# Windowed attention and a gated convolution layer: the first two units' softmax in six parts of two blocks, with other PSUM banks and other planned times

## The chip, the core and the metric

The kernel runs on one core of one Trainium2 chip. The metric is the device time of one execution in microseconds (us); the median of three runs stands for a kernel. The engines are named as in the profile: PE is TensorE (matrix products), PEld its weight loads, DVE is VectorE, ACT is ScalarE, POOL is GpSimd, SP is SyncE, which here only issues transfers (DMA).

## What is computed

```python
def _attn_ref(q, k, v):                       # [8, 8, 576, 64] each
    scores = scale * np.matmul(q, k.transpose(0, 1, 3, 2))
    mask = (rel >= 0) & (rel < 64)            # rel = query place - key place
    scores = np.where(mask, scores, -1000000000.0)
    scores = scores - np.max(scores, axis=-1, keepdims=True)
    attn = np.exp(scores)
    attn = attn / (np.sum(attn, axis=-1, keepdims=True) + 1e-09)
    return np.matmul(attn, v)
...
def _moe_ref(x, w_in, conv_w, w_out):         # x [8, 576, 512], w_in [512, 1024]
    h = np.maximum(x @ w_in, 0.0)
    ...
    for k in range(3):                        # over neighbouring tokens, zeros at a sequence's ends
        conv_out += conv_w[k][None, None, :] * hp[:, k:k + S, :]
    gate = 1.0 / (1.0 + np.exp(-conv_out))
    return h * gate @ w_out
```

Each token attends to itself and the 63 before it, in 8 heads of 64. The three weight arrays come as 64-bit floats, everything else as 32-bit floats.

## The kernel before

**Units.** The 8 x 576 tokens are cut into 12 units (`u`) of 384 tokens, six blocks of 64. For each unit the kernel makes the attention output, splits it in a high and a low half (`xh`, `xl`), multiplies by `w_in`, applies the three-tap convolution and the gate, splits the gated values (`gh`, `gl`) and multiplies by `w_out`.

**The two large products.** Both weights are split in high and low parts too (`wih`, `wil`, `woh`, `wol`), and every product is the sum of three: high by high, high by low, low by high. `mm1` (L512) makes one of eight output strips `f` of a unit with 12 products into a bank of `acc`; `mm2` (L574) adds one strip `f` into the four banks `po` with 12 more. That is 2 x 8 x 12 products a unit, 2304 in all. `relu` on ACT empties `acc` into `hbuf`, of which there are two, so unit u+2 writes over what unit u left. A pair of strips then goes through `conv_mid` (ACT), `conv_side` (DVE, four instructions), `sig` (ACT), `gate` (DVE), `gate_hi` (ACT) and `gate_lo` (DVE), with two buffers `c` and three of `gh` and `gl`.

**Weights.** Each strip of `w_in` arrives as 512 KB of raw 64-bit words in `bits` (`weights`, L258). `to_f32` (L246) makes floats of them with two ACT and three DVE instructions (L250 to L256), POOL or ACT copies out the high half, and a DVE subtraction (L274) leaves the low half `wil` or `wol`. Strips 0 and 1 go alone, later ones in pairs. `mm1` of strip f can't run before its `wil` is there.

**Attention.** A unit has two groups `g` of heads with six blocks each, twelve in all, taken in three sets `b` of four. Scores (`qk`) go to PSUM, DVE takes the row maxima and adds the mask (`row_max`, L363), ACT makes the exponentials and their sums (`exps`, L373), POOL adds 1e-9 to the sums (`guard`, L376), DVE inverts them (L379) and multiplies (`normalise`, L384). In units 0 and 1 PE then transposes the result into `po` (`transpose_pe`, L390) and ACT copies it to `ub` (`untile`, L395); in later units DVE and transfers do that. `values` (L495) multiplies by v into a bank of `acc`, and `split_hi` (ACT, L499) and `split_lo` (DVE, L502) leave `xh` and `xl`. All four strips of `xl` are needed before the first `mm1` of a unit can end. In units 0 and 1 a set of four blocks uses two PSUM banks: for unit 0 those are `sc`, then `po` 2 and 3, then `po` 0 and 1; for unit 1 always `sc`.

**Order.** Nothing is ordered by the loop nest. Every step is put in a list with a due time (`at`, L220), an engine, a cost and the names that it reads and writes; due times come from the table `START` (L139), in units of one `mm1` strip. `queued` (L59) goes through the list with its own costs and writes each engine's instructions in one fixed order, which the chip then follows; each engine works its queue in that order and waits where a name isn't ready. Where PE would stand idle early on, `keep_busy` (L209) puts in products of a zero tile `spare` (L214) that nobody reads.

The two entries that say most about that order:

```python
    "lag": (5.734, 4.983, 5.01, 5, 4.601, 6.631),    # mm2 of strip f is due so many strips after mm1 of it
    "sig": ((5.726, 6.552, 8.72, 10.544), ...        # the sigmoid of pair i is due so many strips after its unit's first
```

Of the kernel before, what the change touches and what calls it, by code (L numbers as in the profile page):

```python
# [30 lines left out]
NBU = 2 * NT // NB  # L31
MASKED = -8.0e9
# [26 lines left out]
def queued(works, fill=None):  # L59
# [80 lines left out]
    "v0": -45.616,  # L140
    "pv0": -37.371,
    "conv": -174.861,
    "bits": ((-210.989, -90.898), (-76.132, -86.24)),
    "qk1": -82.37,
    "lag": (5.734, 4.983, 5.01, 5, 4.601, 6.631),
    "mid": (0.325, 6.316, 0.269, 99),
    "v1": -1.517,
    "qk2": -29.766,
    "qk0": (-93.532, -87.041, -82.642),
    "ex0": (-76.037, -72.861, -50.81),  # L150
    "sc1": (-59.709, -43.924, -30.076),
    "ex1": (-36.764, -20.322, -18.147),
    "mask": -51.623,
    "sig": ((5.726, 6.552, 8.72, 10.544), (1.673, 4.482, 8.678, 7.763), (4.834, 5.504, 8.278, 8.811), (4.046, 6.806, 8.285, 10.314)),
    "in": (-91.819, -70.332, -46.356, -13.522, -9.317),
    "out": (5.121, 7.311, 7.45, 11.284),
# [13 lines left out]
def attention_moe(ctx: ExitStack, tc: tile.TileContext, q, k, v, w_in, conv_w, w_out, out):  # L170
# [57 lines left out]
    def load_qk(t, u, gs=(0, 1)):  # L228

        for g in gs:  # L230
            c, n = slice(2 * g, 2 * g + 2), (4, 2)[g] * W
            cut = (0, n + W, NX + W), (0, n, NX)
            for a in ((0, 1), (1, 2)) if u == 0 else ((0, 2),):
                for name, sb, dram, ends in (("k", ks, k, cut[0]), ("q", qs, q, cut[1])):
                    e = slice(ends[a[0]], ends[a[1]])
                    at(t, "SP", 0.5, lambda c=c, e=e, sb=sb, dram=dram: nc.sync.dma_start(sb[:, c, e], dram[u, :, c, e]),  # L236
                       w=[(name, g, i) for i in range(*a)], mb=(0.00145 if u == 0 else 0.00112) * (e.stop - e.start))
# [66 lines left out]
    def wide(u):  # L304
        return u < BY_PE
# [31 lines left out]
    def halves_of(name, i):  # L337
        return [(name, i, 0), (name, i, 1)]

    def banks_of(u, b):  # L340
# [410 lines left out]
```

## Time and profile before

| | before |
|---|---|
| median of 3 runs | 522.91 us (520.26 to 523.6) |
| the profiled execution's own time | 519.87 us |
| its span, first to last instruction | 517.9 us |
| granted TensorE clock, mean | 0.998 |
| first `mm1` product starts | 34.88 us |
| first `mm2` product starts | 66.77 us |
| DVE busy, 34.9 to 59.4 us | 24.10 of 24.5 us |
| DVE busy, 250 to 450 us | 145.76 of 200 us |

Times in the profile count from the span's first instruction. A row of the timeline gives the start, the length, the engine, the line, the operation, what it writes and reads with shapes, how many instructions are merged, and in brackets how long the engine stood idle before it and what ended that. Instructions of one engine overlap at their ends, so the cost of one among others is the distance to the next one's start. The chain of waits goes back from the last instruction; its pieces don't overlap. In a row of busy times by stretch the columns are the length, the busy time of PE, PEld, DVE, ACT and POOL with instruction counts, the granted clock, the share of the DMA engines and GB/s.

### The profile page before, as it was taken

How to read it: one execution, taken by the hardware profiler on the slowest of the kernel's cores; microseconds unless marked ns; L12 is line 12 of the kernel's file. 1: busy time of each engine (PE TensorE's matmuls, PEld its weight loads, DVE VectorE, ACT ScalarE, POOL GpSimd, SP SyncE). 2: the span in 40 equal slices, each digit the busy share in tenths (PEclk: the TensorE clock that was granted, in tenths of full speed). 3: DMA queues.
4: the chain of work that ended last, by engine and by line, in shares of the span. 5: the costliest groups of instructions: out<-in, count | busy, mean ns of one | idle time of the engine just before them, and what ended most of it. 6: DMA issues, size and time to landing. Idle time of an engine off the chain costs nothing.

```text
span 517.9 us, 14661 instructions
## 1 busy us (share of the span) xinstructions
PE 508.0 (98%) x5742; PEld 488.4 (94%) x5742; DVE 372.4 (72%) x1084; ACT 382.8 (74%) x1015; POOL 85.4 (16%) x186
## 2 busy tenths in 40 slices
PE   9899899999999999999999999999999999999996
PEld 8788899999999999999899999899899999999996
DVE  4799998986787785766668877677677578554550
ACT  5989797979995894894796895795795696444440
POOL 7123131003030120130121130130130021000000
PEclk9999999999999999999999999999999999999999
DMA  8974923152382461462272451362272043010011
GB/s 294 380 274 171 350 80 117 62 176 76 127 291 69 145 218 47 138 208 66 96 255 60 161 202 49 123 234 55 86 260 65 3 153 121 1 62 2 0 62 61
DMA packets 29460, 69.95 MB, mean 135 GB/s; under 512 B 5712, under 2 KB 17616, under 8 KB 29392
## 3 DMA queue, kind: packets, MB, share of 16 engines
q1 hardware_dynamic: 29392, 69.03, 39.3%
q8 instruction: 45, 0.74, 0.6%
q14 instruction: 23, 0.19, 0.1%
HBM read 47.73 MB, written 9.47 MB: 110 GB/s over the span
## 4 chain that ended last, share of the span: by engine, by line
PE 82%; DVE 9%; DMA 5%; ACT 1%; issue 1%; SPq 1%; ACTq 0%
PE po L580 38%; PE acc L515 33%; PE acc L495 6%; PE sc L356 5%; DMA q<-in_q_dram 2%; DVE s L363 2%; DMA bits<-in_w_out_dram 1%; DVE s L384 1%; DVE T L252 1%; DVE T L256 1%; DMA k<-in_k_dram 1%; DVE c L563 1%; DVE wil L274 1%; DVE xl L502 1%; SPq L236 1%
## 5 line engine op out<-in xcount | busy, mean ns | idle before, releaser
L580 PE MATMUL po<-gh,woh 128*128 128x386 f32 (+1 forms) x384 | 132.4, 345 | 0.0
L515 PE MATMUL acc<-xh,wih 128*128 128x384 f32 x384 | 130.7, 340 | 0.6 <-ACT hbuf L534 0.6
L580 PE MATMUL po<-gh,wol 128*128 128x386 f32 (+1 forms) x384 | 130.0, 339 | 0.0
L580 PE MATMUL po<-gl,woh 128*128 128x386 f32 (+1 forms) x384 | 129.7, 338 | 0.1
L515 PE MATMUL acc<-xh,wil 128*128 128x384 f32 x384 | 129.0, 336 | 0.3 <-issue 0.3
L515 PE MATMUL acc<-xl,wih 128*128 128x384 f32 x384 | 128.8, 335 | 0.0
L551 DVE SCALAR_TENSOR_TENSOR c<-hbuf,cw,c 128x386 f32<-128x386 f32 (+1 forms) x192 | 111.9, 633 | 22.5 <-ACT c L544 22.4
L373 ACT ACTIVATE s<-s,nm 128x96 f32<-128x96 f32 (+2 forms) x288 | 105.1, 368 | 3.4 <-DVE nm L363 3.2
L580 PEld LDWEIGHTS po<-gh,woh 128*128 128x128 f32 x384 | 72.2, 188 | 2.9
L515 PEld LDWEIGHTS acc<-xh,wih 128*128 128x128 f32 x384 | 72.1, 188 | 2.7 <-ACT hbuf L534 1.1
L580 PEld LDWEIGHTS po<-gl,woh 128*128 128x128 f32 x384 | 72.4, 188 | 0.4 <-DVE gl L571 0.4
L515 PEld LDWEIGHTS acc<-xh,wil 128*128 128x128 f32 x384 | 72.1, 188 | 0.5 <-issue 0.5
L580 PEld LDWEIGHTS po<-gh,wol 128*128 128x128 f32 x384 | 72.2, 188 | 0.0
L515 PEld LDWEIGHTS acc<-xl,wih 128*128 128x128 f32 x384 | 72.1, 188 | 0.0
L563 DVE TENSOR_TENSOR c<-c,hbuf 128x772 f32<-128x772 f32 (+1 forms) x48 | 47.0, 982 | 31.2 <-ACT c L558 30.8
L571 DVE TENSOR_TENSOR gl<-c,gh 128x772 fp32r<-128x772 f32 (+1 forms) x48 | 51.8, 1082 | 22.1 <-ACT gh L567 21.8
L384 POOL TENSOR_TENSOR s<-s,r 128x768 f32<-128x768 f32 x27 | 40.4, 1496 | 152.1 <-DVE r L379 138.8
L363 DVE CUSTOM_DVE_ANT_0 s<-sc,mask 128x96 f32<-128x96 f32 (+2 forms) x272 | 51.9, 257 | 16.8 <-PE sc L356 16.8
L373 ACT ACTIVATION_READ_ACCUMULATOR s<-s,nm 128x1 f32 x288 | 54.6, 190 | 0.0
L558 ACT ACTIVATE c<-c 128x772 f32<-128x772 f32 (+1 forms) x48 | 40.6, 847 | 18.8 <-DVE c L551 18.6
L567 ACT CAST gh<-c 128x772 fp32r<-128x772 f32 (+1 forms) x48 | 40.0, 834 | 18.4 <-DVE c L563 13.7
L544 ACT ACTIVATE c<-hbuf,cw 128x386 f32<-128x386 f32 (+1 forms) x96 | 53.5, 608 | 0.0
(63 smaller groups left out, 551.9 us busy)
## 6 DMA issues: line engine op xcount, KB each, us to landing
v<-in_v_dram SPq DMA_DIRECT2D x24, 768.0 KB, 6.4
ub<-T SPq DMA_DIRECT2D x240, 48.0 KB, 1.9
k<-in_k_dram SPq DMA_DIRECT2D x22, 448.0 KB, 6.2
q<-in_q_dram SPq DMA_DIRECT2D x22, 384.0 KB, 7.0
out_dram<-T SPq DMA_DIRECT2D x8, 772.0 KB, 3.8
bits<-in_w_in_dram SPq DMA_DIRECT2D x8, 512.0 KB, 6.1
bits<-in_w_out_dram SPq DMA_DIRECT2D x8, 512.0 KB, 6.6
out_dram<-T SPq DMA_DIRECT2D x3, 768.0 KB, 4.6
```

Of the source, the lines that this page charges most:

```text
L363: nc.vector.tensor_tensor_reduce(out=ss[b][:, i, h, o:n], in0=banks_of(u, b)[h][:, i * P + o:i * P + n], in1=mask[m][:, o:n], scale=-0.125 ...
L373: nc.scalar.activation(x, x, AF.Exp, bias=nms[b][:, e], scale=-1.0, accum_out=sms[b][:, e])
L384: on.tensor_tensor(sv, sv, rs[b].unsqueeze(2).broadcast_to([P, 2 * NB, n]), ALU.mult)
L495: nc.tensor.matmul(acc[bank(("v", u, c))][h * D:(h + 1) * D, t * W:(t + 1) * W], vs[:, c, t, h], ub[g][:, 2 * p:2 * p + 2, 2 * t + h], sta ...
L515: nc.tensor.matmul(acc[bank(("m", u, f))][:, :NX], w[:, f, c], x[u % 2][:, c], start=(c == 0 and j == 0), stop=(c == NC - 1 and j == 2))
L544: nc.scalar.activation(cs[i % 2][:, a, :n], hbufs[u % 2][:, f, 1:1 + n], AF.Copy, scale=cw[:, 1, f:f + 1])
L551: nc.vector.scalar_tensor_tensor(c, hbufs[u % 2][:, f, e:e + n], cw[:, e, f:f + 1], c, op0=ALU.mult, op1=ALU.add)
L558: nc.scalar.activation(c, c, AF.Sigmoid)
L563: nc.vector.tensor_tensor(c, c, hbufs[u % 2][:, 2 * i:2 * i + 2, 1:1 + n], ALU.mult)
L567: nc.scalar.copy(ghs[ring(u, i)][:, :, :n], cs[i % 2][:, :, :n])
L571: nc.vector.tensor_tensor(gls[ring(u, i)][:, :, :n], cs[i % 2][:, :, :n], ghs[ring(u, i)][:, :, :n].bitcast(F32), ALU.subtract)
L580: nc.tensor.matmul(po[o][:, :n], w[:, f, es], x, start=(f == 0 and j == 0), stop=(f == NF - 1 and j == 2))
```

## The change

Units 0 and 1 lose `softmax`; in its place `scores` and `weigh` work in six parts of two blocks. `scores` plans the score products and row maxima of one part; `QK_AT` names its banks (-1 is `sc`, 0 is `po` 0 and 1, 2 is `po` 2 and 3). `weigh` plans exponentials, guard, reciprocal, normalisation, transposes and copies for a group of parts: parts 0 and 1 together, 2 alone, 3 alone, 4 and 5 together. So there are four guards, reciprocals and normalisations a unit where there were three; blocks, maxima, exponentials, transposes and copies keep their number. `PE_AT` names the bank of `po` for each part's transposes. The loads of q and k are cut after two of six blocks in both groups (before: after four in the first group, two in the second). The planner knows `po` banks by one name each where it had two halves. All due times in `START` are new; `lag` goes from about 5 to 16 to 18, which puts `mm2` two units behind `mm1`.

```diff
+NP = 2 * NBU
+CUTS = ((2, 6), (2, 6))
+GROUPS = ((0, 1), (2,), (3,), (4, 5))
+QK_AT = (((-1,), (0,), (2,), (-1,), (0,), (2,)), ((-1,), (2,), (-1,), (2,), (-1,), (2,)))
+PE_AT = ((0, 1, 2, 3, 0, 1), (0, 1, 0, 1, 0, 1))
...
-    "lag": (5.734, 4.983, 5.01, 5, 4.601, 6.631),
+    "lag": (16.159, 16.007, 16.941, 17.14, 18.073, 17.348),
...
-    "sig": ((5.726, 6.552, 8.72, 10.544), (1.673, 4.482, 8.678, 7.763), (4.834, 5.504, 8.278, 8.811), (4.046, 6.806, 8.285, 10.314)),
+    "sig": ((12.206, 13.508, 18.787, 21.562), (12.436, 17.352, 18.346, 20.414), (14.01, 17.284, 19.69, 20.122), (15.611, 16.37, 18.929, 20.186)),
...
+    def scores(u, n, t):
+
+        b, bl = n // 2, range(n % 2 * 2, n % 2 * 2 + 2)
+        for i in bl:
+            if block(u, b, i)[1]:
+                at(t - 0.1, "POOL", 0.2, lambda i=i: nc.gpsimd.memset(ss[b][:, i, :, :W], 0.0), w=[("s", b, i)])
+        at(t, "PE", 0.45, lambda: qk(u, b, bl), r=needed(b, bl), w=keys_of(u, b, bl[0]), kind="tiled")
+        for i in bl:
+            at(t + 0.002 + 0.001 * (i % 2), "DVE", 0.42, lambda i=i: row_max(u, b, (i,)),
+               r=keys_of(u, b, i) + ["mask0"], w=[("s", b, i), ("nm", b, i)])
+
+    def weigh(u, ns, t):
+
+        bis = [divmod(2 * n + i, NB) for n in ns for i in range(2)]
+        for b, i in bis:
+            at(t, "ACT", 0.78, lambda b=b, i=i: exps(u, b, i), r=[("nm", b, i)], w=[("s", b, i), ("sm", b, i)], kind="exp")
+        t += 0.45
+        b = bis[0][0]
+        e = slice(2 * bis[0][1], 2 * bis[-1][1] + 2)
+        sw, sr = [("sm", b, i) for _, i in bis], [("s", b, i) for _, i in bis]
+        at(t, "POOL", 0.6, lambda: guard(b, e, nc.gpsimd), w=sw)
+        at(t, "DVE", 0.15, lambda: reciprocal(b, e), r=sw, w=[("r", b, i) for _, i in bis])
+        two(t, "DVE", 0.05 + 0.275 * len(bis), lambda: normalise(u, b, e, nc.vector), r=[("r", b, i) for _, i in bis], w=sr)
+        for n in ns:
+            m, g = [("po", PE_AT[u][n])], 2 * n // NT
+            at(t + 0.4, "PE", 0.66, lambda n=n: transpose_pe(u, n), r=[("s", b, n % 2 * 2), ("s", b, n % 2 * 2 + 1), "mask0"], w=m)
+            at(t + 0.5, "ACT", 0.55, lambda n=n: untile(u, n), r=m, w=[("u", g, i) for i in range(4)])
...
-    for b in range(NBU):
-        softmax(0, b, START["qk0"][b], START["ex0"][b])
+    for n in range(NP):
+        scores(0, n, START["qk0"][n])
+    for ns in GROUPS:
+        weigh(0, ns, START["ex0"][ns[-1]])
```

What the table does is seen in the order of the instructions. PE, just ahead of the first `mm1` (`s_81` holds the first four blocks of unit 1's softmax, `ub_62` the second group of unit 0's). Before:

```order
L495 MATMUL acc_107<-ub_62,v 64x64 x12
L495 MATMUL acc_108<-ub_62,v 64x64 x12
L214 MATMUL po_111<-spare 128x112 x3
L390 MATMUL po_109<-ident,s_81 128x128 x4
L390 MATMUL po_110<-ident,s_81 128x128 x4
L515 MATMUL acc_107<-xh_63,wih 128x384
```

and now, where the score rows of parts 4 and 5 of unit 1 are shown by the last two of part 5:

```order
L522 MATMUL acc_107<-ub_62,v 64x64 x12
L522 MATMUL acc_108<-ub_62,v 64x64 x12
...
L371 MATMUL po_111<-k,q 64x128
L371 MATMUL po_112<-k,q 64x128
L219 MATMUL po_109<-spare 128x112 x2
L542 MATMUL acc_107<-xh_63,wih 128x384
```

The transposes of unit 1 moved from ahead of the first `mm1` to behind it, and all of unit 1's scores stand ahead of it in both.

DVE, around the last two `xl` of unit 0 (`T` is the weights' work buffer, `wil` a low half of `w_in`). Before:

```order
L256 ISA T<-bits_103,T 128x2048
L384 TENSOR_TENSOR s_81<-s_81,r_90 128x1024
L502 TENSOR_TENSOR xl_65<-acc_107,xh_63 128x384
L502 TENSOR_TENSOR xl_65<-acc_108,xh_63 128x384
...
L274 TENSOR_TENSOR wil<-T,wih 128x1024
```

and now:

```order
L262 ISA T<-bits_102,T 128x1024
L529 TENSOR_TENSOR xl_65<-acc_107,xh_63 128x384
L529 TENSOR_TENSOR xl_65<-acc_108,xh_63 128x384
...
L399 TENSOR_TENSOR s_81<-s_81,r_90 128x1024
L394 RECIPROCAL r_91<-sm_88 128x4
...
L399 TENSOR_TENSOR s_82<-s_82,r_91 128x512
L280 TENSOR_TENSOR wil<-T,wih 128x512
L280 TENSOR_TENSOR wil<-T,wih 128x1024
```

The normalisation of unit 1 moved behind `xl`, and so did the low half of weight strip 1 (the row of 512), which before was made long ahead.

PE, where the first `mm2` stands (`gh_95` is the first pair's gated half; `po_109` is the first of four banks). Before, after strip 1 of unit 1 was half done:

```order
L515 MATMUL acc_108<-xl_66,wih 128x384
L580 MATMUL po_109<-gh_95,woh 128x386
...
L580 MATMUL po_112<-gl_98,woh 128x386
L515 MATMUL acc_108<-xh_64,wih 128x384
```

and now, after all eight strips of unit 1:

```order
L542 MATMUL acc_108<-xl_66,wih 128x384
L607 MATMUL po_109<-gh_95,woh 128x386
...
L607 MATMUL po_112<-gl_98,woh 128x386
L522 MATMUL acc_107<-ub_61,v 64x64 x12
```

All 192 `mm1` products of the first two units now stand ahead of the first `mm2`, where 114 did.

More of the change, by code (lines that the diff above doesn't have):

```diff
@@ L456, in softmax @@
+        sw, sr = [("sm", b, i) for i in range(NB)], [("s", b, i) for i in range(NB)]
         if u < 3:
-            at(t, "POOL", 0.6, lambda b=b: guard(b, nc.gpsimd), w=sw)
+            at(t, "POOL", 0.6, lambda: guard(b, e, nc.gpsimd), w=sw)
         else:
-            at(t, "DVE", 0.15, lambda b=b: guard(b, nc.vector), w=sw)
-        at(t, "DVE", 0.15, lambda b=b: reciprocal(b), r=sw, w=[("r", b)])
-        sr = [("s", b, i) for i in range(NB)]
+            at(t, "DVE", 0.15, lambda: guard(b, e, nc.vector), w=sw)
@@ L466, in softmax @@
         t += 0.4
-        if u < BY_PE:
-            for j in range(2):
-                m, g = halves_of("po", (2 * b + j) % NC), place_of(b, NB // 2 * j)[0]
-                at(t, "PE", 0.66, lambda b=b, j=j: transpose_pe(b, j), r=sr + ["mask0"], w=m)
-                at(t + 0.1, "ACT", 0.55, lambda b=b, j=j: untile(b, j), r=m, w=[("u", g, i) for i in range(4)])
-            return
         t = max(t, when[-1][2] + 0.1)
```

136 lines of the change are left out of this document (69 added, 67 removed), and 6 rows, old and new, of the table START.

## The prediction

> **What bounds the kernel now.** The page comes first: the span, and the chain that ended last by engine.
>
> ```profile
> span 517.9 us, 14661 instructions
> ...
> PE 82%; DVE 9%; DMA 5%; ACT 1%; issue 1%; SPq 1%; ACTq 0%
> ```
>
> PE ends the kernel, but a DVE and a DMA part lie on the chain. Where, the busy times by stretch say (PE, PEld, DVE, ACT, POOL; then clock, DMA share, GB/s).
>
> ```profile
> 22.20:34.90 12.70, 11.41 (x183) 9.83 (x183) 11.29 (x52) 10.07 (x38) 2.93 (x3) 1.00 0.75 259
> 34.90:59.40 24.50, 22.93 (x444) 20.26 (x441) 24.10 (x84) 21.93 (x63) 7.63 (x16) 1.00 0.71 265
> 59.40:77.00 17.60, 17.60 (x161) 17.00 (x158) 17.21 (x37) 16.89 (x35) 4.11 (x9) 1.00 0.42 145
> 77.00:120.00 43.00, 42.25 (x431) 40.31 (x431) 37.35 (x84) 35.71 (x80) 2.95 (x8) 1.00 0.40 130
> ...
> 250.00:450.00 200.00, 200.00 (x2398) 193.41 (x2397) 145.76 (x443) 153.80 (x413) 32.76 (x55) 1.00 0.37 125
> ```
>
> To 59 us DVE has hardly a gap; from there PE has none but 0.75 us. The timeline of PE shows when useful work starts, and the rates.
>
> ```profile
> 31.78 1.62 PE L495 MATMUL acc<-ub,v 128*64 128x64 f32 x48
> ...
> 34.09 1.04 PE L390 MATMUL po<-ident,s 128*128 128x128 f32 x8
> 34.88 0.42 PE L515 MATMUL acc<-xh,wih 128*128 128x384 f32 x1
> ...
> 37.15 0.99 PE L356 MATMUL sc<-k,q 64*32 64x96 f32 x64
> ...
> 66.77 0.33 PE L580 MATMUL po<-gh,woh 128*128 128x386 f32 x1
> ...
> 73.08 0.44 PE L515 MATMUL acc<-xh,wih 128*128 128x384 f32 x1
> ```
>
> And from the chain over the whole span, in the steady part and at the end:
>
> ```profile
> 199.64 2.12 PE acc L515 x12
> 201.76 2.10 PE po L580 x12
> ...
> 496.89 16.96 PE po L580 x96
> ```
>
> A strip of 12 products takes 2.10 us, 0.175 a product, whichever of the two it is. From 34.88 us on PE works almost without pause, so the end can only move by what the head gives, or by what new pauses take. The measure: how many of the 2304 large products are done at a given time. By the order, 114 `mm1` stand ahead of the first `mm2`, then 24 `mm2` and 6 `mm1`, and from 73.08 to 76.9 us run 3.8 us of `mm1`, some 20.5 with the change-overs: 164.5 in all.
>
> **The start, to the first mm1.** The chain of waits in the head:
>
> ```profile
> 9.54 11.57 DMA q<-in_q_dram
> ...
> 21.15 1.07 PE sc L356 x32
> ...
> 22.50 0.20 DVE s L363
> 22.70 0.01 DVE nm L363
> ...
> 24.55 0.14 DVE s L363
> ...
> 26.50 1.14 DVE T L252
> ...
> 31.48 1.13 DVE T L256
> 32.62 1.14 DVE s L384
> 33.75 0.93 DVE xl L502 x2
> ```
>
> Unit 1's q lands at 21.11 us, its first row maximum runs at 22.2, the last `xl` of unit 0 ends at 34.7. Between those two DVE also normalises `s_83` of unit 0 and `s_81` of unit 1 and makes two passes over weights: four times 1.14 us that now stand elsewhere. Now there are 16 maxima there, 14 of 128 columns at 0.21 and two of 64 at 0.15 (3.2 us), the weight pass of strip 1 (half of 1.13, 0.6) and four `xl` (1.9): 5.7 us.
>
> When does that stretch start? Two things set it. The transfers:
>
> ```profile
> 7.00:15.00 8.00, 8.00 (x139) 7.16 (x138) 6.62 (x53) 6.36 (x33) 4.37 (x27) 1.00 1.05 384
> ...
> bits<-in_w_in_dram SPq DMA_DIRECT2D x8, 512.0 KB, 6.1
> ```
>
> The DMA engines are full at 384 GB/s. On SP one 512 KB strip more stands ahead of unit 1's q (five where four did): 1.3 us, so q lands at 22.4 and the first maximum can run at 23.4. The other is ACT, which now has all 24 exponentials ahead of the first `untile`, then the first pass over strips 2 and 3.
>
> ```profile
> 16.71 0.56 ACT L395 COPY ub<-po 128x512 f32<-128x512 f32 x1
> ...
> 19.00 1.05 ACT L395 COPY ub<-po 128x512 f32<-128x512 f32 x2
> ...
> 20.72 1.13 ACT L250 ACTIVATE T<-bits 128x1024 f32<-128x1024 f32 x1
> ```
>
> A copy among others costs 0.47 us, a pass over two strips 1.04. The strips now stand behind both loads of v; up to the landing of q at 21.1 the queue before moved 6104 KB, up to that of strip 3 it now moves 4736 (strip 0, all of unit 0's q and k, both v, strips 2 and 3). That is 1368 KB less, 3.5 us at 384 GB/s: 17.6. Pass 1.04, three copies 1.4, the pass over strip 1 0.56, a copy 0.47, the other pass over strips 2 and 3 1.0: 22.1 us. Then DVE's third pass over them, 1.13: 23.4. Both ways give 23.4; 5.7 more, and the last `xl` of unit 0 ends at 29.1 where it ended at 34.7. That gain of 5.6 us is not yet the kernel's: work was put behind it.
>
> **From there to the second unit.** Up to the last `xl` of unit 1 DVE now has these rows: 12 full-width weight passes and normalisations (1.14 each, 13.7), three shifts L251 (0.56, 1.7), three pieces of half width (1.8), 6 maxima of 128 columns, 2 of 64 and 32 of 96 (7.2), four `xl` (1.9), and normalisations of 768, transposes, reciprocals and the convolution's small weights (4.4, an estimate by their widths): 30.7 us. The widths not shown yet:
>
> ```profile
> 36.98 0.65 DVE L251 TENSOR_SCALAR T<-T 128x1024 uint32<-128x1024 uint32 x1
> 37.53 1.22 DVE L384 TENSOR_TENSOR s<-s,r 128x1024 f32<-128x1024 f32 x1
> 38.67 0.26 DVE L363 CUSTOM_DVE_ANT_0 s<-sc,mask 128x96 f32<-128x96 f32 x1
> ...
> 40.09 1.23 DVE L252 SCALAR_TENSOR_TENSOR T<-bits,T 128x1024 uint32<-128x1024 uint32 x1
> ```
>
> (0.55 from the first to the second; eight maxima of 96 in 1.42.) PE follows DVE in this stretch, so each DVE wait counts. Two are added. The first is the low half of strip 1, now behind its copy on POOL, and a POOL copy beside a normalisation is slow:
>
> ```profile
> 32.69 1.96 POOL L273 CAST wih<-T 128x1024 fp32r<-128x1024 f32 x1 [5.21 <-DVE T L256]
> ...
> 45.46 1.04 POOL L273 CAST wih<-T 128x1024 fp32r<-128x1024 f32 x1 [1.08 <-DVE T L256]
> ```
>
> The first of these ran beside the normalisation at 32.62, the second did not: 0 to 0.9 us, and I take 0.9, since the two again stand side by side. The Trainium skill has the rule for it (SBUF — State Buffer, Terms, "shared port pair": DVE and GpSimd lock it for a whole instruction, the loser waits). By that rule the split into four normalisations gives a guard four chances a unit to be held for up to one of them; the trace bears out the hold, and the sum would lose at most another 1.1 us.
>
> The second wait is what DVE idled in the same stretch before (24.10 of 24.50): 0.4. So the last `xl` of unit 1 ends at 29.1 + 30.7 + 0.9 + 0.4 = 61.1 us. Strips 0 to 7 of unit 0 are done by then: their 16.8 us, four `values` of 0.8, four score groups of 0.95 and the transposes, 0.4 a part and 2.4 in all, make 26.2 us of PE work between 29.1 and 61.1. Of unit 1 only the second half of strip 0 and seven strips remain, 90 products, 15.75 us with nothing to wait for but ACT. At 76.9 us 192 products are done, against 164.5: 27.5 x 0.175 = 4.8 us ahead. Scores, values and transposes done are the same in both at that time, and so the 0.9 us of transposes that went behind the first `mm1` is in it.
>
> **After that** PE has all it needs if the gates keep up. The first pair's `gl` comes 13.9 us of DVE rows after the last `xl` of unit 1, at 75.0, and is wanted at 76.9. The third pair's comes 37.1 us after it, at 98.2; PE wants it after 4.2 + 2.6 + 1.1 + 0.5 of `mm2`, 10.5 of `mm1`, four `values` (3.2) and two score groups (1.9), at 100.9. Both margins are about 2 us: the cover is there, and thin. In the steady part the work per unit is the same, the number of product groups changes little, and the tail is the same copy and transfer behind PE's last product. Two entries cost nothing: one name for a bank instead of two removes no instruction, and the spare products that go, 16 of 63 rows, lie where PE waits.
>
> The sum: 517.9 - 4.8 = 513.1 us of span. The profiled execution took 519.87 us, 2.0 more than its span; the median of the runs shown is 522.91, another 3.0. The same 4.8 from the median: 518.1.
>
> **Rivals.**
>
> *More is gained* (0.17). If POOL's copy meets no normalisation, DVE doesn't idle, and the strips land with the first v (768 KB, 2.0 us earlier, with q at 22.4 still the later end, so 0 from that), 0.9 + 0.4 return, and the 0.75 us that PE lost from 77 to 120 may go, a few shorter regroupings on PE besides: 6.1 to 7.5, median 516.1. For it: 24.10 of 24.5 shows how few gaps DVE can have.
>
> *The head gives less* (0.24). ACT's fixed order puts copies that PE waits for behind strips still in transit. Each microsecond that strips 2 and 3 land later than 17.6 moves 23.4 and all behind it; the 6.1 us from issue to landing is a median under such load. With 2 us later, or the same lost in the thin margins up to 100 us, 2.8 remain; with 4.8, none: median 520.1 to 522.9.
>
> *Slower* (0.13). `relu` of unit u+2 may not write `hbuf` before `gate` of unit u has read it, and with `mm2` two units behind, the gate is near that limit in every unit. The chain of one pair is 0.6 + 0.6 on ACT, four `conv_side`, `sig` and `gate`. From the group means,
>
> ```profile
> L551 DVE SCALAR_TENSOR_TENSOR c<-hbuf,cw,c 128x386 f32<-128x386 f32 (+1 forms) x192 | 111.9, 633 | 22.5 <-ACT c L544 22.4
> L558 ACT ACTIVATE c<-c 128x772 f32<-128x772 f32 (+1 forms) x48 | 40.6, 847 | 18.8 <-DVE c L551 18.6
> L563 DVE TENSOR_TENSOR c<-c,hbuf 128x772 f32<-128x772 f32 (+1 forms) x48 | 47.0, 982 | 31.2 <-ACT c L558 30.8
> ```
>
> 1.2 + 2.5 + 0.85 + 1.0 = 5.6 us. For the fourth pair PE gives it about six strips, 13 us, from the freeing of its `c` to the next use of the `acc` bank. DVE is busy 29 of 40 us a unit, so in 13 us it has 9.4 of work, 3.5 of it this pair's; 5.9 of others' plus 5.6 is 11.5. From 1.5 us more on PE pauses in each of ten units; 1 us each is 10 us: 513.1 + 10, median 528.1. Against it: a quarter of DVE is free, and what `relu` waits for is PE:
>
> ```profile
> ACT hbuf L538 <- PE acc L515: 27.5, 24, 2.6
> ```
>
> *The clock* (0.03). Fewer spare products before the first `mm1` could let the granted clock fall; one strip at half clock costs 2.1 us, median 520.2. Before, the clock is 1.00 in each stretch quoted. The Trainium skill (TensorE: Matmul & The Clock Gate, What's actually happening) has the clock halved after an idle window of about 3.4 us; no run here shows that.
>
> **Chances and range.** The forecast as summed, 3 to 6 us gained, has 0.43. A median of three runs of this kernel tells 1% (5.2 us) from no change at best. Faster by over 1% is the rival with more gain and two fifths of the forecast: 0.35. Slower is 0.13; the rest, 0.52, is within 1%. The range goes from 514.5 (a gain of 7.5 and 1 us of scatter) to 523.5 (no gain, and some scatter); the slower rival and some of the clock's lie outside. The forecast's own range is 516.9 to 519.9.
>
> **What would show it.** First `mm1` near 29 us and its last `xl` at 29.1; last `xl` of unit 1 at 61; first `mm2` at 77; no pause of PE over 0.5 us from 61 on. A first `mm2` at 80 or later says the head gave less; PE waiting for `hbuf` or `gl` in every unit after 120 us is the slower rival. The forecast is wrong at its root if the stretch before 61 isn't carried by DVE's rows, or PE's steady rate isn't 0.175.

## The result, and the profile after

The changed kernel takes 517.08 us (median of 15 runs, 515.53 to 520.81) where the kernel before takes 520.52 on the same chip (15 runs, 519.0 to 523.6). The ratio is 0.9936, with a 95% interval of 0.9913 to 0.9958: 3.3 us gained, 2.2 to 4.5 by the interval. Beside the last experiment the changed kernel was timed again: 516.98 against 519.96, ratio 0.9952 (0.9933 to 0.9971). The profiled execution took 516.12 us, its span is 3.6 us shorter than before's. The 522.91 us from which the forecast started is the median of the first three of before's 15 runs, 2.4 us above the median of all.

From the page of the changed kernel, the span and the chain by engine:

```profile
span 514.3 us, 14601 instructions
...
PE 89%; DVE 5%; ACT 2%; DMA 2%; issue 0%; SPq 0%; DVEq 0%; ACTq 0%
```

PE's share of the chain rose from 82 to 89%, DVE's fell from 9 to 5% and that of DMA from 5 to 2%: less of the chain lies on DVE's rows and on transfers. The busy times by stretch of the changed kernel (PE, PEld, DVE, ACT, POOL; then clock, DMA share, GB/s):

```profile
22.20:29.40 7.20, 6.64 (x148) 5.81 (x152) 6.83 (x39) 6.64 (x26) 1.90 (x3) 1.00 0.87 294
29.40:61.00 31.60, 29.82 (x557) 27.02 (x555) 30.30 (x117) 29.94 (x107) 9.12 (x21) 1.00 0.71 251
...
77.00:120.00 43.00, 41.32 (x623) 39.37 (x623) 38.17 (x134) 37.37 (x117) 8.89 (x14) 1.00 0.47 150
120.00:250.00 130.00, 130.00 (x1439) 126.40 (x1438) 89.65 (x262) 101.01 (x263) 23.01 (x40) 1.00 0.40 131
250.00:450.00 200.00, 199.97 (x2279) 193.83 (x2278) 137.42 (x405) 146.65 (x379) 31.26 (x53) 1.00 0.36 114
```

Up to 61 us DVE has little room, and so has ACT (29.94 of 31.6 us, which the prediction did not look at). After 120 us PE is full, as before. But from 77 to 120 PE now lacks 1.68 us where it lacked 0.75. The timeline of DVE in the head, and of PE from the first `mm1` on:

```profile
23.86 0.28 DVE L378 CUSTOM_DVE_ANT_0 s<-sc,mask 128x128 f32<-128x128 f32 x1
...
28.63 1.02 DVE L529 TENSOR_TENSOR xl<-acc,xh 128x384 fp32r<-128x384 f32 x2
...
32.98 1.83 DVE L280 TENSOR_TENSOR wil<-T,wih 128x512 fp32r<-128x512 f32 x2
...
38.16 0.69 DVE L257 TENSOR_SCALAR T<-T 128x1024 uint32<-128x1024 uint32 x1 [1.17 <-ACT T L256]
...
60.98 0.55 DVE L529 TENSOR_TENSOR xl<-acc,xh 128x384 fp32r<-128x384 f32 x1
61.45 0.95 DVE L399 TENSOR_TENSOR s<-s,r 128x768 f32<-128x768 f32 x1
```

```profile
30.32 0.42 PE L542 MATMUL acc<-xh,wih 128*128 128x384 f32 x1
...
33.59 0.99 PE L371 MATMUL sc<-k,q 64*32 64x96 f32 x64 [0.94 <-DMA q<-in_q_dram]
...
77.53 0.33 PE L607 MATMUL po<-gh,woh 128*128 128x386 f32 x1
...
83.55 1.62 PE L522 MATMUL acc<-ub,v 128*64 128x64 f32 x48 [1.64 <-ACT hbuf L561]
```

The last row is the new pause: 1.64 us, waiting for a `relu` of ACT to free `acc`. What ACT did then:

```profile
79.10 1.15 ACT L256 ACTIVATE T<-bits 128x1024 f32<-128x1024 f32 x1 [2.11 <-DMA bits<-in_w_out_dram]
...
83.04 0.83 ACT L561 ACTIVATE hbuf<-acc 128x384 f32<-128x384 f32 x2
```

ACT stood 2.11 us in front of strips of `w_out` still in transit. The two `relu`, whose products PE had ended at 75.6 and 77.7, are behind that pass, a gate copy and six exponentials in ACT's order.

The sum goes like this. At 77.53 us the changed kernel has done 192 large products. The kernel before had 164.5 at 76.9, so 168.1 at 77.53, and 23.9 products of 0.175 us are 4.2 us. Counted in the traces it is 23, since the kernel before has begun 169 by then; the score and value products still to come are the same in both, 1600 and 960. To 120 us the changed kernel loses 0.93 us more than the one before (1.68 - 0.75), and after that neither loses anything. That leaves 3.3 of the 3.6 us between the two spans; where the rest comes from was not traced.

### The profile page after: what moved, and what is told of

Same layout as the page of the kernel before. It is cut to its first block, busy times and chain, and to the rows that moved or that the text cites. A ratio compares the mean times of both kernels' runs of the same rounds, so it can differ in the third digit from the quotient of the medians.

```text
span 514.3 us, 14601 instructions
## 1 busy us (share of the span) xinstructions
PE 504.4 (98%) x5710; PEld 487.0 (95%) x5710; DVE 367.0 (71%) x1088; ACT 380.0 (74%) x1013; POOL 91.2 (18%) x188
## 4 chain that ended last, share of the span: by engine, by line
PE 89%; DVE 5%; ACT 2%; DMA 2%; issue 0%; SPq 0%; DVEq 0%; ACTq 0%
PE po L607 40%; PE acc L542 36%; PE acc L522 6%; PE sc L371 5%; DVE s L378 2%; PE acc L219 1%; DMA bits<-in_w_out_dram 1%; DVE T L262 1%; ACT T L256 1%; DMA q<-in_q_dram 1%; PE po L371 1%; DVE wil L280 1%; DVE s L399 1%; ACT ub L409 0%; DVE xl L529 0%
## 5 line engine op out<-in xcount | busy, mean ns | idle before, releaser
L399 POOL TENSOR_TENSOR s<-s,r 128x768 f32<-128x768 f32 x27 | 41.8, 1547 | 231.0 <-DVE r L394 180.4
L598 DVE TENSOR_TENSOR gl<-c,gh 128x772 fp32r<-128x772 f32 (+1 forms) x48 | 47.3, 986 | 22.8 <-ACT gh L594 21.9
L378 DVE CUSTOM_DVE_ANT_0 s<-sc,mask 128x96 f32<-128x96 f32 (+2 forms) x260 | 49.1, 254 | 16.0 <-PE sc L371 15.5
L565 ACT ACTIVATE hbuf<-acc 128x384 f32<-128x384 f32 x64 | 30.9, 484 | 28.3 <-PE acc L542 28.3
```

Source lines behind the costliest of these rows:

```text
L378: nc.vector.tensor_tensor_reduce(out=ss[b][:, i, h, o:n], in0=bank_of(u, b, i, h)[:, o:n], in1=mask[m][:, o:n], scale=-0.125, scalar=3.0e3 ...
L399: on.tensor_tensor(sv, sv, rs[b][:, e].unsqueeze(2).broadcast_to([P, e.stop - e.start, n]), ALU.mult)
L565: nc.scalar.activation(hbuf[:, f, o:o + NX], ps[:, :NX], AF.Relu)
L598: nc.vector.tensor_tensor(gls[ring(u, i)][:, :, :n], cs[i % 2][:, :, :n], ghs[ring(u, i)][:, :, :n].bitcast(F32), ALU.subtract)
```

## The experiments

In the kernels of this table the order of the engines is that of the changed kernel except for the instructions named, because the edit moves them in the planner's finished list. Where planned times or the code of the parts change, the planner orders everything anew. The kernels were timed on several chips, each beside the kernel before, so the ratios compare better than the medians.

| kernel | median us | ratio to before (95%) | first `mm2` at, us | span behind it, us |
|---|---|---|---|---|
| changed kernel | 517.08 | 0.9936 (0.9913 to 0.9958) | 77.53 | 436.8 |
| the same, again | 516.98 | 0.9952 (0.9933 to 0.9971) | 76.86 | 437.8 |
| relu first | 516.42 | 0.9929 (0.9916 to 0.9943) | 78.28 | 437.4 |
| strips first | 516.14 | 0.9930 (0.9912 to 0.9948) | 79.28 | 435.6 |
| scores behind | 516.24 | 0.9930 (0.9906 to 0.9954) | 78.42 | 436.2 |
| both moves | 515.95 | 0.9928 (0.9902 to 0.9954) | 81.38 | 436.7 |

The last two columns are from each kernel's one profiled execution. "Scores behind" has the strips moved too.

### What the pause at 83.5 us costs

First the two `relu` were moved on ACT:

```diff
...
+late = [x for x in order if x.eng == "ACT" and x.t < 16 and x.w in ([("h", 1, 6)], [("h", 1, 7)])]
+order = [x for x in order if x not in late]
+i = next(n for n, x in enumerate(order) if x.eng == "ACT" and x.t == START["out"][3])
+order[i:i] = late
...
```

> The changed kernel with two entries of ACT's order moved: the relu of the last two strips of unit 1 stand ahead of ACT's pass over the strips of w_out that land at 79 us, and so ahead of a gate copy and six exponentials too; nothing else moves. Theory (the head gave what was forecast, and 1.64 us of it was lost again at 83.55 because ACT stood in front of a transfer): the pause of PE at 83.5 goes to under 0.3 us, the span falls from 514.3 to 512.7 us, 5.2 below before's 517.9, and the median by as much (515.4 where the changed kernel has 517.1). Rival (the margins behind are used up: what PE takes next, the low halves of the gate or the weights, is late anyway): the pause turns up a few us later, span within 0.5 of 514.3.

Measured: 516.42 us, and a span of 515.7 in the profile. The pause was not gone but had moved by one step of PE's order. PE and ACT of this run:

```profile
85.51 1.16 PE L371 MATMUL sc<-k,q 64*32 64x96 f32 x64 [1.30 <-DVE nm L378]
```

```profile
80.23 1.12 ACT L256 ACTIVATE T<-bits 128x1024 f32<-128x1024 f32 x1 [1.25 <-DMA bits<-in_w_out_dram]
```

Now PE waits for row maxima, which stand behind the same weight pass in DVE's order. The rival was right for this run: PE's 77 to 120 us hold 41.32 us of work again. (Only its span missed the rival's figure, since in this execution PE also waited 2.46 us for unit 2's q at 39.8.) So not ACT's order alone but the landing of the strips is the cause, and the next run moves that. On SP, k and q of unit 3 were issued ahead of those strips:

```diff
...
+late = [x for x in order if x.eng == "SP" and 15 < x.t < 15.9 and x.w and x.w[0][0] in ("k", "q") and x.w[0][1] == 0]
+order = [x for x in order if x not in late]
+i = max(n for n, x in enumerate(order) if x.eng == "SP" and x.w and x.w[0][:2] == ("bits", 1))
+order[i + 1:i + 1] = late
...
```

> The changed kernel with one move in SP's order: the two strips of w_out that ACT waits for at 79 us are issued ahead of k and q of unit 3 (832 KB) instead of behind them; PE, DVE, ACT and POOL as in the changed kernel. Theory (ACT and DVE both stood in front of that transfer, and so the last relu and the next row maxima came late): the strips land about 2 us earlier, at 77 (832 KB at the 400 GB/s moved there), PE's pause at 83.5 goes, and with it no other one of over 0.5 us appears up to 120 us; 1.6 us off the span of a like execution, median about 515. Rival (the strips are late because their buffer comes free late, or the other transfers slow them all the same): they land within 0.5 us of 79, and the time is that of the changed kernel.

The strips landed at 78.96 in an execution whose first `mm2` was 1.75 us later than that of the changed kernel, so 1.9 us earlier against the rest of the work. By the absolute time alone this is what the rival had said; from the issue on SP to ACT's pass it now took 5.2 us instead of 6.7. ACT and the stretch of PE:

```profile
78.96 1.14 ACT L256 ACTIVATE T<-bits 128x1024 f32<-128x1024 f32 x1 [0.21 <-DMA bits<-in_w_out_dram]
```

```profile
77.00:120.00 43.00, 42.79 (x633) 40.91 (x632) 39.70 (x134) 39.06 (x122) 10.62 (x14) 1.00 0.51 168
```

PE lacks 0.21 us where it lacked 1.68, and the span behind the first `mm2` is 1.2 us shorter. The pause is gone by the mechanism named, and it stays away in the two other profiles with this move ("scores behind" and "both moves"), where ACT doesn't wait for these strips at all. The median, 516.14, is 0.9 under that of the changed kernel, or 0.3 by the ratios, which these two intervals do not tell from nothing. The head of this execution was late, with 1.84 us of waiting for unit 2's q at 40.8, and hid the gain in the span. Both moves together were therefore timed beside the changed kernel on one chip:

> The changed kernel itself, beside the run below on the same chip: 517.1 us as before, pause of PE of 1.6 us near 83.5.

> The changed kernel with both moves that bear on the pause at 83.5: the strips of w_out ahead of k and q of unit 3 in SP's order, and the last two relu of unit 1 ahead of ACT's pass over them. Theory (1.2 to 1.6 us of the forecast gain were lost at that place, and the rest of what was missing is scatter of the transfers in the head): no pause of PE over 0.5 us between 77 and 120, the part of the span behind the first mm2 under 435.9 us (changed kernel 436.8), median 1.2 to 1.6 under that of the changed kernel on the same chip. Rival (the head's scatter hides it, or the place costs less than its pause): under 0.6 us.

The changed kernel showed its pause again:

```profile
82.83 1.62 PE L522 MATMUL acc<-ub,v 128*64 128x64 f32 x48 [1.59 <-ACT hbuf L561]
```

With both moves PE waits 0.40 us between 77 and 120. The medians are 515.95 and 516.98: 1.0 us apart, between what theory (1.2 to 1.6) and rival (under 0.6) gave, with intervals that overlap. The 436.7 us behind the first `mm2` miss the expected 435.9. In that execution the clock was halved for a while in the head (below), but that lies ahead of the first `mm2` and doesn't explain it. That the place holds PE for 1.6 us is shown; that its removal shortens the run by 0.3 to 1.2 us, as the three ratios have it, is likely and not settled. This version has the lowest median of all, but it isn't told from the changed kernel.

### Whether DVE's rows in the head move the end

Three idle products, expected at 0.86 us each, were put on DVE ahead of unit 1's first maximum, on top of the kernel with the `relu` moved:

```diff
...
+i = next(n for n, x in enumerate(order) if x.eng == "DVE" and x.t == START["sc1"][0] + 0.002)
+unused = cs[0].rearrange("p a n -> p (a n)")[:, :6 * P].rearrange("p (a n) -> p a n", n=P)
+m0 = mask[0].unsqueeze(1).broadcast_to([P, 6, P])
+for _ in range(3):
+    order.insert(i, Work(0, "DVE", 1.14, lambda: nc.vector.tensor_tensor(unused, m0, m0, ALU.mult), [], [], None, 0, 0.0))
```

> The kernel of the run above, with three extra DVE products of 768 columns (0.86 us each, 2.6 in all; their output is used by nothing) just ahead of unit 1's first row maximum. Theory (up to 61 us the order of DVE's rows sets when PE gets its strips, from there PE never waits, so the end moves one for one): the last xl of unit 0 ends at 32.2 instead of 29.6, the first mm1 is at 32.9, the first mm2 at 80.1, the span 2.6 over that of the run above (515.3). Rival (transfers and ACT set the pace of the first two units, and DVE has room): the last xl of unit 1 moves by under 1 us, and the span by under 1.

Measured: 520.68 us, 4.3 more than without the delay (4.1 by the ratios, 1.0008 against 0.9929), and the first `mm1` at 35.86 instead of 32.9. Both theory and rival missed, for two reasons. The delay was longer than planned: from the first of the three products to the next row DVE took 3.57 us, 1.19 each, not 0.86.

```profile
23.74 3.65 DVE L719 TENSOR_TENSOR c<-mask 128x768 f32<-128x768 f32 x3
27.31 0.28 DVE L378 CUSTOM_DVE_ANT_0 s<-sc,mask 128x128 f32<-128x128 f32 x1
```

Wherever the expectations say 2.6 us of delay, 3.57 were put in. And something else came in. PE, and the stretches by the microsecond, of this run:

```profile
28.08 1.33 PE L371 MATMUL sc<-k,q 64*64 64x128 f32 x16 [3.40 <-DVE nm L378]
```

```profile
27.00:28.00 1.00, 0.00 (x0) 0.00 (x0) 1.00 (x8) 0.30 (x1) 0.00 (x0) 0.58 0.96 340
28.00:29.00 1.00, 0.92 (x16) 0.92 (x16) 1.00 (x13) 1.00 (x7) 0.00 (x0) 0.50 0.54 213
...
33.00:34.00 1.00, 1.00 (x22) 0.88 (x22) 0.56 (x1) 0.20 (x2) 0.44 (x1) 0.51 0.26 90
```

PE idled 3.40 us for DVE, and the granted clock (the column behind the engines) fell to 0.50 for 6.8 us. A first try to keep PE busy with 24 spare products took a bank that DVE had still to read:

> The run with the three extra DVE products (2.6 us) again, with 24 spare products more on PE just ahead of the score part for which PE then waited 3.40 us, so that PE isn't idle for more than 1 us there. Theory (two costs were mixed: DVE's rows, one for one, and a granted clock that falls to 0.50 for 6.6 us once PE has idled about 3 us): the clock stays 1.00 through 22 to 36 us, the first mm1 is 2.6 us later than in the run without the delay (near 32.7), and the median 2.6 over it (519). Rival (the clock fell for another reason): clock at 0.50 again around 28 to 34 us, median 520.7 as before.

The spare products themselves waited, and the try failed:

```profile
27.84 9.60 PE L219 MATMUL po<-spare 128*128 128x112 f32 x60 [4.80 <-DVE nm L378]
```

PE idled 4.80 us, the clock fell to 0.50 again, the spare products ran 9.6 us, and the median was 528.76. It says nothing on DVE's rows. The second try lengthened the spare products that stand there, in their own bank, from 6 to 17, and was made on the kernel with the strips moved:

```diff
...
+j = next(n for n, x in enumerate(order) if x.eng == "PE" and x.t == START["sc1"][2])
+order.insert(j, Work(0, "PE", 0, keep_busy(11, ("po", 0)), [], [], None, 0, 0.0))
...
```

> The delay of three DVE products (2.6 us) ahead of unit 1's first row maximum once more, on the kernel with the strips moved (516.1), with the spare products ahead of the third score part of unit 1 lengthened from 6 to 17, in the bank they are in already, so that PE has no idle time near 3 us. Theory (DVE's rows ahead of the first mm1 move the end one for one, and what the earlier delay cost beyond 2.6 us was the halved clock): clock 1.00 between 22 and 40 us, first mm1 near 33.3, median 2.6 over, 518.7. Rival (one microsecond of DVE there costs PE more, since PE's and ACT's orders stand behind it too): median 520 or above with the clock at 1.00.

```profile
22.20:29.40 7.20, 6.94 (x119) 6.45 (x117) 7.10 (x10) 3.84 (x7) 1.90 (x2) 1.00 0.67 217
29.40:61.00 31.60, 31.21 (x562) 28.00 (x563) 31.60 (x146) 31.25 (x119) 8.19 (x20) 1.00 0.71 251
```

The clock stayed at 1.00 there, and the mean clock of the other 11 executions was 0.997 to 1.000, where it was 0.991 to 0.997 with the first delay. The median is 518.14 us: 2.0 more than 516.14, or 2.5 by the ratios (0.9978, 0.9952 to 1.0005, against 0.9930, 0.9912 to 0.9948); these intervals allow 0.8 to 4.2. DVE in its profile:

```profile
25.45 3.65 DVE L721 TENSOR_TENSOR c<-mask 128x768 f32<-128x768 f32 x3
29.02 0.28 DVE L378 CUSTOM_DVE_ANT_0 s<-sc,mask 128x128 f32<-128x128 f32 x1
...
33.80 1.01 DVE L529 TENSOR_TENSOR xl<-acc,xh 128x384 fp32r<-128x384 f32 x2
34.73 0.28 DVE L378 CUSTOM_DVE_ANT_0 s<-sc,mask 128x128 f32<-128x128 f32 x1
```

The three products took 3.57 us again, and from the first maximum to the end of the last `xl` of unit 0 it is again 5.7 us (29.02 to 34.73), with the first `mm1` at 35.11. So up to there DVE's rows count one for one. For the end of the kernel that isn't shown: 3.57 us lie within the interval, but the value found is 2.0 to 2.5. A part may be taken up by waits that DVE had anyway: without the delay it idled 1.87 us between 29.4 and 61 us (29.73 busy of 31.6), here it is busy 31.60 of 31.6, so an estimate from these two profiles is 3.57 - 1.87 = 1.7 us. This profile is a late one, though: its execution took 523.15 us, with transfers late from the start and the clock at 0.50 from 8.2 to 15.1 and from 93.6 to 97.0 us. Of the 1.8 us by which its first `mm1` missed the expected 33.3, the longer delay is 1.0. The first delay cost 1.6 us more than the second by the ratios (2.3 by the medians), which fits the halved clock; the intervals do not tell it from nothing.

### Parts alone, times alone

The changed code with before's planned times (each part with the time of its block):

> The changed code (six parts, four normalisations, the new cuts and banks) with the planned times of before, each part taking the time of its block. By its order, the rows of DVE from unit 1's first maximum to the last xl of unit 0 make 9.2 us (before 10.9, changed kernel 5.7), those from there to the last xl of unit 1 25.6 (25.0 and 30.5), and 108 mm1 stand ahead of the first mm2 (114 and 192). Theory (the gain is DVE work moved behind unit 0's last xl, which the times do): first mm1 near 33.5, 0 to 1.5 us gained on before, median 519 to 520.5. Rival (the finer cut itself gives the gain): median as the changed kernel, 517.1, or lower.

The code of before with the changed kernel's times (two of the replaced entries are shown; where the changed code has two times for a block, the later one):

```diff
-    "qk0": (-93.532, -87.041, -82.642),
-    "ex0": (-76.037, -72.861, -50.81),
+    "qk0": (-91.793, -77.793, -77.835),
+    "ex0": (-78.229, -55.953, -50.944),
```

> The code of before (three blocks of four, its banks and cuts) with the planned times of the changed kernel, a block taking the later time of its two parts. By its order the rows of DVE from unit 1's first maximum to the last xl of unit 0 make 7.5 us, those to the last xl of unit 1 34.3, and 192 mm1 stand ahead of the first mm2. Theory (the times do it): last xl of unit 0 near 31, that of unit 1 near 66, first mm2 near 78, two thirds of the changed kernel's gain: 2 to 3 us, median 517.5 to 518.5. Rival (without the parts the new times are worth nothing): median 520.5 or above.

Both are slower than before: 526.33 us (1.0114, 1.0093 to 1.0136) and 532.71 (1.0233, 1.0212 to 1.0254). Theory and rival both missed, and not in the head. In the first, the last `xl` of unit 0 ended at 32.1 us and the first `mm1` came at 32.16 (expected 33.5). Then PE and ACT show:

```profile
42.96 0.66 PE L404 MATMUL po<-ident,s 128*128 128x128 f32 x4 [3.27 <-ACT ub L409]
```

```profile
41.31 1.12 ACT L256 ACTIVATE T<-bits 128x1024 f32<-128x1024 f32 x1 [3.78 <-DMA bits<-in_w_in_dram]
```

This is the mechanism of 83.5 us at another place: ACT in front of a strip, and the copy that PE needs behind it. PE idled 3.27 us, and the clock was 0.50 for 6.8 us after it. In the second, the last `xl` of unit 0 ended at 31.0 (expected 31) and that of unit 1 at 67.2 (66); PE and DVE:

```profile
66.60 0.56 DVE L502 TENSOR_TENSOR xl<-acc,xh 128x384 fp32r<-128x384 f32 x1
```

```profile
84.37 0.33 PE L580 MATMUL po<-gh,woh 128*128 128x386 f32 x1
```

PE began unit 1's eight strips only at 66.93, behind 12 spare products; their 96 products of 0.175 are 16.8 us, and a wait of 0.38 and the change-overs bring it to 84.37. So the 78 of my expectation was a slip: it left out a step that the prediction has, the 90 products (15.75 us) behind the last `xl`, which from 66 gives 81.75. DVE's rows had given the last `xl` to about 1 us. Behind the first `mm2` it needs 444.3 us where the changed kernel needs 436.8, 3.75 of them spare products that the planner now put there.

The third kernel of this kind makes three sets of the four for the normalisations:

```diff
-GROUPS = ((0, 1), (2,), (3,), (4, 5))
+GROUPS = ((0, 1), (2, 3), (4, 5))
```

> The changed kernel with three sets for the normalisations (parts 0 and 1, 2 and 3, 4 and 5) instead of four; the planner then orders what is behind anew: by its order DVE has the same 5.7 us from unit 1's first maximum to the last xl of unit 0, 32.6 instead of 30.5 to the last xl of unit 1, and 180 mm1 stand ahead of the first mm2 instead of 192. Theory (the rows ahead of the last xl of unit 0 set the gain): first mm1 within 0.5 us of the changed kernel's 30.3, the time within 2 us of it (515.5 to 519). Rival (the fourth set, which lets the transposes of part 2 start before part 3 is weighed, makes the gain): first mm1 1 us or more later, median as before the change, 520.

Measured: 523.62 us (1.0078, 1.0054 to 1.0102). The first `mm1`, at 30.00, came as the theory had it. But the last `xl` of unit 1 ended at 63.6 instead of 61.45, PE waited 1.20 us for a transfer and 2.38 us for an `xl` later (94.33 and 98.33), and the clock was at 0.50 for 3.4 us after that. So the time missed both ranges. I had taken "the times carry the gain", with "the parts carry it" as the rival; both fall. Each of the three has its first `mm1` 2.7 to 5.4 us ahead of before's and loses more than that behind it: the first where ACT stands in front of a strip and the clock falls, the second in DVE's rows up to the last `xl` of unit 1 and in spare products, the third in PE's two waits and the clock. How much the parts and how much the times are worth can't be told apart by these kernels.

### Banks, and the transfer of unit 2's q

All score parts in one pair of banks, in the changed kernel's order:

```diff
-        j = pair(u, NB * b + i)
-        return (sc[h] if j < 0 else po[j + h])[:, i % 2 * P:(i % 2 + 1) * P]
+        return sc[h][:, i % 2 * P:(i % 2 + 1) * P]
```

> The changed kernel, all instructions in its order, but every score part of the first two units goes to the one pair of banks sc, so that the products of a part wait for the maxima of the part before. Theory (DVE's rows carry the stretch from 23.9 to 29.6, and the banks let PE run ahead of them): between two parts DVE now waits for half of PE's 0.6 us and the handing over, some 0.8 us, three times in unit 1 ahead of the last xl of unit 0: first mm1 near 32.7, the span 2.5 over the changed kernel's, median 519.5; up to 5 if unit 0 loses as much. Rival (the banks were not needed: transfers and ACT keep the parts apart anyway): median within 0.7 of 517.1.

This did not make the waits that I wanted. The order has the products of two parts one behind the other ahead of the maxima, so the second part's scores overwrite the first's, the maxima of some parts read the scores of the next part, and this kernel leaves the right softmax out. PE does both parts in one go:

```profile
22.02 1.00 PE L370 MATMUL sc<-k,q 64*64 64x128 f32 x32
```

Its first `mm1` is at 30.36, its median 519.58 (0.9998, 0.9978 to 1.0017). What the banks are worth stays open.

Last, on the kernel with the strips moved, two score groups of unit 2 were put later on PE, since PE waited for unit 2's q at 33.6 us, and in other profiles for the second half of it too, 1.84 us at 40.8 and 2.46 at 39.8. (At 38.9 the changed kernel's trace names a DVE pass, not q, as what ended the 0.76 us.)

```diff
...
+for key, last in ((("k", 0, 1), 2), (("k", 1, 1), 3)):
+    x = next(x for x in order if x.eng == "PE" and x.kind == "eight" and key in x.r)
+    n = order.index(x) + 1
+    while last:
+        last -= order[n].eng == "PE"
+        n += 1
+    order.insert(n, x)
+    order.remove(x)
...
```

> The kernel with the strips ahead of k and q of unit 3, and in PE's order two score groups of unit 2 stand later: the first behind the two transposes that follow it, the second behind a transpose and two half strips of mm1. Theory (in 29 to 61 us the loss is not DVE's rows but the transfer of unit 2's q, which PE meets too early, and the transposes, copies and DVE's next weight pass stand behind it): PE's waits for q at 33.6 (0.94 us) and 38.9 (0.76 by the changed kernel's profile, up to 2.46 in other profiles) go, DVE's idle 1.17 us at 38 goes, the first mm2 is 1.5 to 2.5 us earlier for the same landing of unit 1's q, and the median falls 1.5 to 2.5 under the 516.1 of the run with the strips moved: 513.6 to 514.6. Rival (DVE carries the stretch by its rows, 30.3 of 31.6 us busy, and the wait for q is hidden by that): under 0.7 us gained.

The rival holds: 516.24 us against 516.14. DVE still waits for ACT at the same place, and PE still for q:

```profile
39.39 0.69 DVE L257 TENSOR_SCALAR T<-T 128x1024 uint32<-128x1024 uint32 x1 [1.36 <-ACT T L256]
```

```profile
34.90 0.99 PE L371 MATMUL sc<-k,q 64*32 64x96 f32 x64 [1.04 <-DMA q<-in_q_dram]
```

Why DVE's wait stayed is seen on ACT, whose weight pass DVE waits for. In the changed kernel ACT idled for a transpose that stands on PE behind the wait for q:

```profile
35.26 0.59 ACT L409 COPY ub<-po 128x512 f32<-128x512 f32 x1 [1.01 <-PE po L404]
```

With the score groups later that is gone, and in its place ACT stands in front of a strip of `w_in` still in transit:

```profile
38.21 1.15 ACT L256 ACTIVATE T<-bits 128x1024 f32<-128x1024 f32 x1 [1.93 <-DMA bits<-in_w_in_dram]
```

So PE's order did hold ACT, and through it DVE, but behind that wait stood the next one, once more a weight pass in front of a transfer. DVE's row began at 39.39, and at 39.00 in the profile with only the strips moved: nothing was gained there.

## Why the prediction was right, and where it was off

The forecast was 4.8 us gained. Measured are 3.3, with 4.8 just outside the interval; the sign and the mechanism hold. That the time itself, 517.08 us, came within 1.0 of the forecast 518.1 is partly luck: the median from which 4.8 was taken off was 2.4 us high, and from 520.52 the same sum gives 515.7. Step by step:

- **"The first maximum can run at 23.4"**: 23.86. **"5.7 more"** of DVE's rows: 23.86 to 29.57, 5.7. The last `xl` of unit 0 ends at 29.57 (29.1). Right, and with a delay of 3.57 us and the clock kept this stretch moved as a whole; the end moved by 2.0 to 2.5. (The second of the two ways to 23.4 sums to 23.2; nothing hangs on that.)
- **"First `mm1` near 29"**: 30.32. PE has the last score part and spare products of unit 1 between; it cost nothing later, since DVE sets the pace to 61 us.
- **The last `xl` of unit 1 at 61.1**: 61.45. The length was right, its parts not quite: the 0.9 us of waiting for POOL's copy did not come (the two low halves at 32.98 run on without idle time), and in its place DVE waited 1.17 us for ACT. The guards were not held either: in units 0 and 1 they took 0.22 to 0.32 us, before 0.24 to 1.44.
- **First `mm2` at 77**: 77.53, so 4.2 us ahead of before instead of 4.8. In the other executions of the same head it came between 76.86 and 81.38.
- **"No pause of PE over 0.5 us from 61 on", "PE has all it needs if the gates keep up"**: this step failed. The gates did keep up (the first pair's `gl` ended at 75.3, forecast 75.0, and PE waits for none up to 120 us). What was late was a `relu` behind a weight pass behind a transfer: 1.64 us at 83.5. The prediction had just that mechanism as the rival "the head gives less", with copies in the head; it came behind the head, where I had looked at DVE's rows and PE's demand only, not at what ACT's and DVE's orders have ahead of them from SP. Strips issued earlier take the pause away. The term mis-sized is this one: 0 forecast, 0.9 net of the pauses that before had there.
- **"Slower"**, the gate of every unit: no. PE is busy 130.00 of 130 us after 120, and it waits for nothing there.
- **The clock**, given 0.03 and one strip's time: it is 1.00 in every stretch of the profiled execution. But 3 of the changed kernel's 21 timed executions had a mean clock of 0.992 or 0.993, and took 519.8 to 520.8 us; of the 62 of before that ran beside the experiments none was under 0.998. As a rival for the median it fell. As a cost it exists, about 3 us in one execution of seven. None of these three has a profile; 0.993 is also the mean clock of the profiled run with the first delay, whose clock was halved for 6.8 us in the head.

## What to carry to other kernels

When a planner freezes the order of each engine, cost a reordering by two lists: the work ahead of the first wait, and at every place where an engine's next entry needs a transfer, what stands behind that entry and who needs it. Moving work behind the head fills the engines there too, and the next wait is found in their orders, not in their busy shares. Planned times tuned for one cut of the work did not carry over to the other here: parts alone and times alone lost some 6 and 13 us where both together gained 3. And when work is put in to test a bound, read its length from the trace before reading the result: 2.6 us were meant here and 3.57 came.

## What the runs showed of the hardware

PE's granted clock fell by half after idle times of 2.0 to 4.8 us, and stayed there for one or two periods of 3.4 us. In the kernel with both moves PE waited 2.84 us:

```profile
35.72 1.15 PE L371 MATMUL sc<-k,q 64*32 64x96 f32 x64 [2.84 <-DMA q<-in_q_dram]
```

```profile
36.00:37.00 1.00, 1.00 (x62) 0.72 (x41) 0.00 (x0) 0.00 (x0) 0.00 (x0) 0.70 1.02 407
...
39.00:40.00 1.00, 1.00 (x5) 1.00 (x4) 0.67 (x3) 1.00 (x4) 0.26 (x1) 0.59 0.07 26
```

Taking 0.50 and 1.00 as the only two values, the clock was halved from 36.40 (0.70 in that microsecond) to 39.82 (0.59): 3.4 us. After 3.27, 3.40 and 4.80 us of idle time (the runs above) it was halved for 6.8 us each time. With the `relu` moved, an idle time of 2.46 us left it at 1.00:

```profile
39.83 0.99 PE L371 MATMUL sc<-k,q 64*32 64x96 f32 x64 [2.46 <-DMA q<-in_q_dram]
```

```profile
40.00:41.00 1.00, 1.00 (x66) 0.85 (x53) 1.00 (x3) 1.00 (x1) 0.00 (x0) 1.00 0.00 0
```

But shorter idle times than that halved it elsewhere: 2.38 us in the kernel with three sets, 2.29 us in the second delay, and 2.01 us early in the head of "scores behind". The last two:

```profile
93.72 2.83 PE L522 MATMUL acc<-ub,v 128*64 128x64 f32 x48 [2.29 <-DMA ub<-T]
```

```profile
93.00:94.00 1.00, 0.28 (x6) 0.31 (x8) 0.14 (x1) 0.00 (x0) 0.00 (x0) 0.78 0.83 301
94.00:95.00 1.00, 1.00 (x24) 1.00 (x23) 0.00 (x0) 0.00 (x0) 0.00 (x0) 0.50 1.12 395
```

```profile
7.10 0.57 PE L371 MATMUL sc<-k,q 64*64 64x64 f32 x16 [2.01 <-DMA q<-in_q_dram]
```

```profile
8.00:9.00 1.00, 1.00 (x7) 0.83 (x6) 1.00 (x9) 0.92 (x5) 0.84 (x3) 0.61 1.13 396
```

So the length of the idle time alone doesn't decide. Its place does: in each of the seven profiles with a fall in mid-run, the falls of the clock, the one behind PE's last product included, lie whole multiples of 3.413 us apart (in the second delay at 8.23, 93.57 and 520.23 us, 25 and 125 periods). If the traces are cut into windows of 3.413 us by these times, from 6.4 us on, and PE's idle time is summed in each, every window with 2.01 us or more ends with the clock at 0.50, and no window with 1.84 us or less makes it fall, but for one that ends at 8.23 us in the second delay (1.50). The 2.46 us above straddle such a time, 38.93, with 1.57 us ahead of it and 0.90 behind, and the clock stayed. A halved clock came back after one window where PE idled 0.15 us or less in that window, and after two where it idled 0.47 us or more.

The fall can come after PE has started again: at 36.4 where PE restarted at 35.72. The Trainium skill (TensorE: Matmul & The Clock Gate, What's actually happening) describes this: two states, set by a free-running window of about 3.4 us. The durations and the distances of the falls agree with such windows. The Trainium skill's section on HAM oscillation, on the same page, gives the rule as no idle gap over about 3.4 us; here 2.01 us were enough.

The landing of unit 2's q scattered more than expected: with the same instructions ahead of it, PE waited 0.94 us for it in one profile and 2.84 in another. In a head whose idle times lie between 2 and 3 us, this can decide whether an execution pays for the halved clock.
